# New step lists and PSUM rooms for a gated linear attention and its maxout layer

## Chip, core and metric

The kernel runs on one core of a Trainium2 chip. The metric is the device time of one launch in microseconds (us). "The median" is that of the runs shown.

## What is computed

Four batches, eight heads, 768 positions, head dimension 48. The attention is a recurrence with a complex gate for each position and channel; its output, turned into 3072 rows of 384, goes through three matrices of 384 x 768, an elementwise maximum and a matrix of 768 x 384. The inputs are float32, the four matrices float64.

```python
mag = np.sqrt(a_re * a_re + a_im * a_im)
scale = np.minimum(mag, 0.999) / (mag + 1e-06)
a_re_n, a_im_n = (a_re * scale, a_im * scale)
for t in range(S):
    ar, ai = (a_re_n[:, :, t, :, None], a_im_n[:, :, t, :, None])
    new_re = ar * S_re - ai * S_im
    new_im = ar * S_im + ai * S_re
    kv = np.einsum('bhd,bhe->bhde', k[:, :, t], v[:, :, t])
    S_re, S_im = (new_re + kv, new_im)
    y[:, :, t] = np.einsum('bhd,bhde->bhe', q[:, :, t], S_re)
...
h = np.maximum(np.maximum(x @ w1, x @ w2), x @ w3)
return (h @ w_out).astype(np.float32)
```

## The kernel before, in words

The recurrence is computed in chunks. A chunk x is 128 positions of one batch with all eight heads; two chunks, called x and y in the step names, form a pair, and there are twelve pairs, 0 to 11. A pair goes through the gates, the scores, the state and the output of the attention, then through the maxout layer and the output matrix. Several pairs are in work at the same time.

All work is cut into steps, and the order of the steps is one list, SCHEDULE, written out by hand or by a planner ahead of time. A word such as `tpqx:5` is a step's name and its pair. The loop `program` calls `run` on each word; each engine gets its instructions in the order of the list, held by manual dependencies (class Bound), so an engine never overtakes itself. The engines still wait for one another's results.

The steps that matter here:

- L.. are loads issued by SyncE (Lr and Li the gate's parts, Lk, Lq, Lv; WL the weights). W with a, b, c, e, g turns float64 weights into float32: a on ScalarE, b, c, e on VectorE, g an accumulating transfer of GpSimd.
- sqr, sqi, add, lnL, expe, expw, lne, relu, Lnop, abs, pw, addw, lnw, expL, mulai, mulw, stt, xor, half, atan and turn make the gate's logarithm and angle on ScalarE and VectorE. Lnop and addw are either accumulating transfers of GpSimd or additions on VectorE. Activations of two table sets alternate, and each change of the set is a table load on ScalarE.
- cs, sums and F are TensorE's running sums of angles and logarithms. t, nf, af, sa and sb turn the angles into sines; En, Ek, Eq and f0 to f3 are exponentials out of PSUM on ScalarE.
- mk, mq, uk, uq and kEn scale k and q on VectorE; tpk and tpq are TensorE's transposes, 16 matmuls each; Kc and Qc copy them out of PSUM. Q1, Q2, QB, KB and QG are further factors on VectorE.
- A and B are score matmuls; g0 to g3 (VectorE) and b0, b1 (ScalarE) put the scores under a mask. dk is the state's matmuls, h0 to h3 add it up. y is the output in PSUM, the steps xx and xy copy it to the tile xhx.
- For pair 0 the maxout layer runs plainly (U01x and so on, O). From pair 1, U01, U11, U02 and U12 are nine matmul blocks each (width 256), and u01 to u12 take the maximum on VectorE, with the first as a relu on either engine. The output matrix uses seven products (Strassen) P1 to P7: S1 to S4 are sums on VectorE, Px and Py a remaining block, and r1, r6, r75, r57, ox and oy collect the products into the tile ot. Dx and Dy store it.

TensorE works with five shapes of its array, here called tiles: 128x128 for up, op, pw, wt and wm; 128x64 for cs; 128x32 for A, B and y; 64x128 for tp; 64x64 for F, sums and dk. In the profile's names "up" are the U steps, "op" the products P and O.

PSUM is used as four rooms of two banks. Each step of TensorE takes the next room from the string SLOTS (digits 0, 2, 4, 6); it waits until what stood there has been read. The set OTHER names the steps made by the other engine of ScalarE and VectorE than usual.

Of the kernel before, what the change touches and what calls it, by code (L numbers as in the profile page):

```python
# [26 lines left out]
turn1:0 nfx:0 Wc9:0 afx:0 Wa10:0 T2:0 sqr:1 sqi:1 sax:0 sbx:0 t2:0 Wc10:0 We9:0 add:1 ukx:0 WL11:0 Lvx:0 uqx:0 We10:0
csy:0 tpkx:0 tpqx:0 lnL:1 ty:0 Kcx:0 Eqy:0 expw:1 kEnx:0 xor:1 nfy:0 Lky:0 Liy:2 Lix:2 WL1:0 WL2:0 Lrx:2 WL4:0 Lvy:0
Lry:2 dkx:0 Fy:0 Wb11:0 relu:1 Qcx:0 expe:1 QBx:0 Q2x:0 mqy:0 abs:1 Wa11:0 Wc11:0 Wb1:0 half:1 lne:1 f2y:0 Eny:0 f1y:0
Eky:0 f3y:0 h1x:0 f0y:0 pw:1 Wa1:0 lnw:1 expL:1 We11:0 Wb2:0 Q1x:0 h2x:0 Wc1:0 h3x:0 QGx:0 Wa2:0 afy:0 say:0 mulai:1  # L30
We1:0 CL:0 Wb4:0 Wc2:0 mulw:1 We2:0 M0:0 M1:0 Zg:0 Lnop:1 Cdx:0 Wg1:0 Cdy:0 Wa4:0 sby:0 sqr:2 sqi:2 sumsx:1 Ax:0 M2:0
Wg2:0 stt:1 Wc4:0 mky:0 atan:1 uqy:0 Ekx:1 Eqx:1 Enx:1 We4:0 add:2 lnL:2 expe:2 relu:2 g0x:0 g1x:0 uky:0 KBx:0 g2x:0
g3x:0 turn:1 m1:0 Bx:0 b0x:0 tpqy:0 tpky:0 m0:0 b1x:0 Kcy:0 WL5:0 Lkx:1 csx:1 csy:1 tx:1 yx:0 xor:2 Qcy:0 Wb5:0 nfx:1
Q2y:0 Q1y:0 ty:1 expw:2 afx:1 Wa5:0 xx:0 abs:2 Ay:0 sax:1 QBy:0 Wc5:0 KBy:0 We5:0 addw:2 kEny:0 nfy:1 g0y:0 g1y:0 g2y:0
g3y:0 Wg4:0 Z4:0 Wg5:0 half:2 Cdx:1 Z3:0 WL7:0 WL8:0 Lqx:1 Lqy:1 Lky:1 U11x:0 sumsy:1 dky:0 By:0 lnw:2 Wb7:0 QGy:0
u11x:0 expL:2 mulai:2 mulw:2 Eny:1 Eky:1 Eqy:1 b0y:0 Wa7:0 h1y:0 b1y:0 afy:1 U02x:0 U01x:0 yy:0 u01x:0 xy:0 sbx:1 say:1
sby:1 h2y:0 Wc7:0 Cdy:1 Z2:0 Lvx:1 h3y:0 stt:2 U12x:0 Liy:3 atan:2 lne:2 We7:0 u12x:0 mkx:1 mqx:1 u02x:0 ukx:1 turn:2
mky:1 uqx:1 Wb8:0 U01y:0 U02y:0 U11y:0 u11y:0 u01y:0 U12y:0 Wa8:0 u02y:0 u12y:0 uky:1 csx:2 tx:2 nfx:2 tpkx:1 tpqx:1
tpky:1 Lnop:2 Wc8:0 We8:0 Wg7:0 Kcx:1 Kcy:1 Qcx:1 U21y:0 Fx:1 sumsx:2 Fy:1 Lix:4 f3x:1 f1x:1 f2x:1 f0x:1 f3y:1 f1y:1
f2y:1 f0y:1 u21y:0 csy:2 kEnx:1 Q1x:1 Wg8:0 ty:2 Eqx:2 Ekx:2 U21x:0 u21x:0 Enx:2 mqy:1 uqy:1 Q2x:1 nfy:2 U22y:0 dkx:1  # L40
tpqy:1 Qcy:1 afy:2 say:2 h0x:1 h1x:1 QBx:1 Ax:1 g0x:1 u22y:0 KBx:1 g1x:1 Lqx:2 Lky:2 Lvy:1 Lkx:2 Lix:3 h0y:1 mqx:2 h2x:1
Q2y:1 h3x:1 Q1y:1 g2x:1 g3x:1 sbx:2 sqi:3 sby:2 afx:2 Oy:0 Fx:2 oy:0 sax:2 Bx:1 b1x:1 b0x:1 Ay:1 QGx:1 yx:1 Lvx:2 Lrx:3
Lry:3 Lqy:2 U22x:0 kEny:1 QBy:1 g0y:1 g1y:1 g2y:1 KBy:1 g3y:1 f2x:2 f3x:2 xx:1 sqr:3 sumsy:2 Eqy:2 f0x:2 f1x:2 add:3
u22x:0 dky:1 By:1 Ox:0 J3:0 mkx:2 h1y:1 b1y:1 Eny:2 Eky:2 lnL:3 expe:3 b0y:1 relu:3 h2y:1 ukx:2 mky:2 uqx:2 xor:3 uky:2
QGy:1 expw:3 ox:0 abs:3 tpkx:2 tpqx:2 kEnx:2 h3y:1 yy:1 Kcx:2 Qcx:2 xy:1 dkx:2 Fy:2 addw:3 mqy:2 Q2x:2 half:3 QBx:2
f1y:2 f0y:2 f3y:2 lne:3 lnw:3 expL:3 f2y:2 uqy:2 h0x:2 KBx:2 Q1x:2 U11:1 u11:1 mulw:3 h1x:2 J1:0 Lnop:3 tpky:2 tpqy:2
kEny:2 Ax:2 Kcy:2 Qcy:2 Lrx:4 Lry:4 Lvx:3 Liy:4 Dx:0 Lvy:2 U01:1 Q1y:2 g0x:2 g1x:2 g2x:2 Q2y:2 g3x:2 mulai:3 h2x:2 h3x:2
Cdy:2 Cdx:2 sumsy:3 Bx:2 u01:1 Ay:2 Fx:3 KBy:2 g0y:2 g1y:2 h0y:2 b0x:2 b1x:2 Eny:3 g2y:2 stt:3 Eqy:3 sqr:4 atan:3 g3y:2
U02:1 U12:1 QGx:2 QBy:2 J2:0 turn:3 sqi:4 f1x:3 f0x:3 f2x:3 f3x:3 add:4 yx:2 u12:1 u02:1 csx:3 csy:3 lnL:4 xx:2 tx:3
xor:4 S1:1 nfx:3 dky:2 sumsx:3 ty:3 nfy:3 h1y:2 Eky:3 expe:4 Enx:3 Eqx:3 expw:4 S2:1 QGy:2 h2y:2 h3y:2 relu:4 afx:3 S3:1  # L50
By:2 Ekx:3 P5:1 P6:1 P1:1 P7:1 sax:3 sbx:3 Lqy:3 Lqx:3 abs:4 mqx:3 afy:3 b0y:2 b1y:2 say:3 r1:1 sby:3 addw:4 lne:4 Lix:5
Dy:0 Lry:5 Lkx:3 Lvx:4 Px:1 P2:1 S4:1 mkx:3 P3:1 Py:1 J4:0 yy:2 xy:2 r6:1 r75:1 uqx:3 ukx:3 Lky:3 mqy:3 uqy:3 r57:1
mky:3 tpkx:3 tpqy:3 tpqx:3 Lrx:5 Lvy:3 Liy:5 h0x:3 Kcx:3 kEnx:3 P4:1 Qcy:3 lnw:4 Qcx:3 uky:3 dkx:3 Fy:3 U11:2 f1y:3
expL:4 f0y:3 Lnop:4 oy:1 Q2x:3 half:4 mulai:4 mulw:4 f3y:3 f2y:3 h1x:3 QBx:3 Q1x:3 ox:1 stt:4 h0y:3 sqi:5 h2x:3 Q1y:3
Cdx:3 Cdy:3 h3x:3 Dy:1 Dx:1 atan:4 sqr:5 add:5 lnL:5 turn:4 Lix:6 Lqy:4 Lry:6 Lrx:6 Lky:4 Lqx:4 U01:2 u01:2 u11:2 U02:2
tpky:3 Kcy:3 csy:4 expe:5 ty:4 relu:5 xor:5 u02:2 S3:2 QGx:3 csx:4 tx:4 expw:5 abs:5 Ax:3 nfy:4 nfx:4 KBx:3 kEny:3 g0x:3
g1x:3 afx:4 U12:2 u12:2 g2x:3 g3x:3 S1:2 Fx:4 f2x:4 f3x:4 f1x:4 f0x:4 sumsy:4 Eny:4 Eqy:4 Eky:4 Lkx:4 dky:3 Lvy:4 Liy:6
sumsx:4 Bx:3 Ekx:4 Eqx:4 S2:2 Q2y:3 mqy:4 h1y:3 addw:5 sby:4 sbx:4 sax:4 b1x:3 b0x:3 h0x:4 h2y:3 KBy:3 h3y:3 mky:4 QBy:3
mkx:4 ukx:4 P7:2 P6:2 P5:2 P1:2 yx:3 Ay:3 xx:3 lnw:5 lne:5 expL:5 r1:2 Enx:4 Px:2 Py:2 P4:2 QGy:3 S4:2 r6:2 g0y:3 g1y:3
g2y:3 g3y:3 afy:4 mulw:5 r75:2 half:5 P2:2 By:3 P3:2 b1y:3 b0y:3 yy:3 say:4 xy:3 r57:2 mqx:4 uqx:4 ox:2 mulai:5 tpqx:4  # L60
tpkx:4 oy:2 kEnx:4 Fy:4 uky:4 Lnop:5 Kcx:4 uqy:4 sumsx:5 U11:3 KBx:4 Lqx:5 Cdx:4 f2y:4 stt:5 f3y:4 Ekx:5 f0y:4 Lkx:5
Dy:2 Dx:2 Qcx:4 Enx:5 Q1x:4 Cdy:4 u11:3 Eqx:5 QBx:4 mkx:5 QGx:4 U01:3 atan:5 Q2x:4 u01:3 f1y:4 h0y:4 U02:3 u02:3 sqr:6
dkx:4 h1x:4 sqi:6 h2x:4 h3x:4 Fx:5 f0x:5 f3x:5 add:6 f1x:5 f2x:5 Ax:4 g0x:4 Lqy:5 g1x:4 Bx:4 lnL:6 expe:6 g2x:4 g3x:4
U12:3 lne:6 b1x:4 tpky:4 turn:5 mqx:5 b0x:4 tpqy:4 Qcy:4 u12:3 kEny:4 S1:3 csy:5 ty:5 csx:5 Kcy:4 dky:4 nfy:5 S3:3
sumsy:5 h1y:4 h2y:4 tx:5 nfx:5 h3y:4 afy:5 yx:4 Eky:5 Eny:5 Eqy:5 afx:5 Q2y:4 Q1y:4 sbx:5 P5:3 P1:3 P7:3 Lky:5 sax:5
Ay:4 xx:4 KBy:4 ukx:5 uqx:5 Lrx:7 tpqx:5 S2:3 expw:6 relu:6 QBy:4 Lnop:6 mky:5 tpkx:5 S4:3 Kcx:5 g0y:4 Qcx:5 P6:3 Px:3
Py:3 r1:3 By:4 P2:3 P4:3 say:5 sby:5 QGy:4 g1y:4 abs:6 g2y:4 g3y:4 b1y:4 b0y:4 KBx:5 mqy:5 r6:3 r75:3 r57:3 kEnx:5 oy:3
Q1x:5 uky:5 xor:6 Lry:7 sqr:7 Fy:5 f2y:5 sumsx:6 uqy:5 f3y:5 yy:4 P3:3 ox:3 f0y:5 Lkx:6 xy:4 QGx:5 addw:6 U11:4 Liy:7
Dx:3 QBx:5 Ekx:6 mkx:6 Enx:6 Lvx:5 f1y:5 lnw:6 Lqx:6 h0y:5 u11:4 Q2x:5 expL:6 mulai:6 mulw:6 U01:4 u01:4 tpky:5 h0x:5
Eqx:6 Kcy:5 tpqy:5 stt:6 Ax:5 Lix:7 atan:6 g0x:5 Qcy:5 g1x:5 g2x:5 Bx:5 kEny:5 g3x:5 b0x:5 Q2y:5 U02:4 sqi:7 b1x:5 add:7  # L70
lnL:7 relu:7 expe:7 u02:4 U12:4 Fx:6 f2x:6 S3:4 f3x:6 half:6 turn:6 f0x:6 u12:4 Lvy:5 dky:5 h1y:5 Q1y:5 f1x:6 sumsy:6
dkx:5 Eny:6 csy:6 csx:6 h1x:5 mqx:6 S1:4 Dy:3 ty:6 nfy:6 S2:4 Eqy:6 Lqy:6 mqy:6 Eky:6 P1:4 KBy:5 tx:6 nfx:6 afx:6 lne:7
expw:7 afy:6 P7:4 abs:7 Lky:6 Ay:5 QBy:5 g0y:5 g1y:5 g2y:5 yx:5 g3y:5 addw:7 sbx:6 sax:6 ukx:6 uqx:6 By:5 say:6 P5:4
xx:5 P6:4 r1:4 r6:4 lnw:7 xor:7 S4:4 half:7 Px:4 P2:4 b0y:5 Py:4 r75:4 P4:4 r57:4 P3:4 expL:7 mulw:7 QGy:5 oy:4 tpqx:6
tpkx:6 b1y:5 Lnop:7 mky:6 Qcx:6 Q1x:6 ox:4 Liy:8 kEnx:6 yy:5 sumsx:7 xy:5 Cdx:6 Enx:7 Fy:6 f2y:6 f0y:6 f3y:6 mulai:7
f1y:6 Eqx:7 QBx:6 QGx:6 Q2x:6 stt:7 Lqx:7 Ekx:7 Lix:8 U01:5 sqi:8 Lry:8 Cdy:6 Kcx:6 Lrx:8 Lvx:6 dkx:6 h1x:6 sby:6 mqx:7
# [966 lines left out]
```

## Time and profile before

| | |
|---|---|
| median of three runs | 557.37 us (556.8 to 559.04) |
| span of the profiled execution, first to last instruction | 553.2 us |
| median less that span | 4.2 us |
| TensorE busy | 523.6 us |
| VectorE busy | 482.1 us |
| ScalarE busy | 368.2 us |
| mean granted clock of TensorE | 0.992 |
| table loads of ScalarE | 49, 62.9 us in all |

The profile shows one execution. Its own time is known by the span, to which the time of launch and end is to be added. A row of a timeline has start, length, engine, line, operation, out<-in, shapes and a count; in square brackets stands the idle time ahead of it and what ended that. Almost every row carries line 201, that of the helper which records the instructions, so rows are told apart by their tiles. A matmul in float32 leaves two records. The rows of matmuls overlap, so distances are taken from start to start.

### The profile page before, as it was taken

Reading aid. Unit: us, or ns where it says so; the run is one execution under the profiler, and the core shown is the slowest. Engines: PE = TensorE matmul, PEld = TensorE weight load, DVE = VectorE, ACT = ScalarE, POOL = GpSimd, SP = SyncE. Lnnn points to the kernel's source line nnn. Section 1 sums busy time; section 2 is a strip of 40 time slices with the busy share of each in tenths; the row PEclk is TensorE's granted clock in tenths of the full one; section 3 lists DMA queues with packets and bytes.
Section 4 is the critical chain, followed back from the end, with each engine's and each line's share of the span. In section 5 each row is a group of like instructions: output and inputs, shape, how many; then the busy total and the mean of one; then the engine's idle time right before and its main releaser. Section 6 shows DMA issues by size and latency. Waiting matters only on the chain.

```text
span 553.2 us, 22687 instructions
## 1 busy us (share of the span) xinstructions
PE 523.6 (95%) x10086; PEld 448.1 (81%) x10086; DVE 482.1 (87%) x752; ACT 368.2 (67%) x653; POOL 70.8 (13%) x113
## 2 busy tenths in 40 slices
...
GB/s 203 295 246 176 174 131 79 50 128 63 109 38 124 67 68 51 61 44 88 72 121 58 35 85 108 101 91 54 62 125 20 32 105 72 2 31 2 31 1 28
...
## 3 DMA queue, kind: packets, MB, share of 16 engines
...
q14 instruction: 18, 0.15, 0.1%
...
## 4 chain that ended last, share of the span: by engine, by line
PE 84%; DVE 7%; ACT 4%; SPq 2%; issue 1%; DMA 1%; DVEq 0%; ACTq 0%
PE up L201 33%; PE op L201 24%; PE y L201 7%; PE A L201 5%; PE tp L201 4%; PE dk L201 3%; PE sums L201 2%; PE cs L201 2%; DVE w L201 2%; SPq L201 2%; PE F L201 2%; PE B L201 1%; DMA wo<-in_moe_w_dram 1%; DVE atm L201 1%; ACT f L201 1%
## 5 line engine op out<-in xcount | busy, mean ns | idle before, releaser
L201 PE MATMUL up<-xhx,w 128*128 128x256 f32 x792 | 177.0, 382 | 0.1
L201 PEld LDWEIGHTS up<-xhx,w 128*128 128x128 f32 x792 | 148.6, 190 | 21.5 <-PE B L201 0.3
L201 ACT ACT_TABLE_LOAD x49 | 62.9, 1283 | 1.6 <-PEq L1027 0.8
L201 ACT COPY atm<-B 32x128 f32<-32x128 f32 x96 | 24.6, 256 | 37.8 <-DVE atm L201 19.7
L201 PE MATMUL op<-wo,xhx 128*128 128x192 f32 (+1 forms) x220 | 48.4, 363 | 0.0
L201 DVE TENSOR_TENSOR Q<-Q,f 112x1024 f32<-112x1024 f32 (+1 forms) x48 | 45.4, 952 | 1.7 <-ACT Q L201 1.2
L201 POOL DMA_DIRECT2D ar<-nf x40 | 34.6, 1305 | 60.3 <-DVE ar L201 48.9
L201 ACT ACTIVATE f<-F 48x232 f32<-48x232 f32 x96 | 34.5, 359 | 10.1 <-PE F L201 6.1
L201 PEld LDWEIGHTS op<-wo,xhx 128*128 128x128 f32 x220 | 36.5, 190 | 4.6 <-issue 0.6
L201 PE MATMUL y<-atm,vb 128*32 128x64 f32 x1152 | 39.0, 221 | 0.2 <-ACT K L201 0.2
L201 PE MATMUL y<-QG,g 112*32 112x64 f32 x1408 | 38.0, 219 | 0.2 <-issue 0.2
L201 PEld LDWEIGHTS y<-atm,vb 128*32 128x32 f32 x1152 | 32.4, 109 | 5.3 <-issue 2.9
L201 PEld LDWEIGHTS y<-QG,g 112*32 112x32 f32 x1408 | 34.8, 109 | 0.3 <-issue 0.3
L201 DVE TENSOR_TENSOR ot<-ot,op 128x384 f32<-128x384 f32 (+1 forms) x56 | 25.6, 464 | 10.7 <-PE op L201 6.4
L201 PE MATMUL op<-wo,strassen 128*128 128x192 f32 x176 | 33.0, 331 | 0.0
L201 POOL DMA_DIRECT2D Ln<-e x9 | 8.3, 923 | 192.2 <-ACT e L201 53.8
L201 PE MATMUL A<-Q,K 112*32 112x80 f32 x1536 | 31.6, 234 | 1.4 <-DVE Q L201 1.4
L201 DVE COPY_PREDICATED atm<-masko,A 128x256 f32<-128x256 uint8 x72 | 31.2, 435 | 1.7
L201 PE MATMUL op<-w,strassen 128*128 128x192 f32 x176 | 32.2, 329 | 0.0
L201 PEld LDWEIGHTS A<-Q,K 112*32 112x32 f32 x1536 | 27.3, 110 | 4.2 <-issue 3.1
L201 PEld LDWEIGHTS op<-wo,strassen 128*128 128x128 f32 x176 | 28.8, 190 | 0.8
L201 ACT COPY Q<-tp 112x1024 f32<-112x1024 f32 x22 | 22.3, 1014 | 10.7 <-PE tp L201 10.5
...
## 6 DMA issues: line engine op xcount, KB each, us to landing
...
Ln<-e POOLq DMA_DIRECT2D x9, 384.0 KB, 4.1
w<-L POOLq DMA_DIRECT2D x7, 384.0 KB, 4.4
```

Of the source, the lines that this page charges most:

```text
L201: ins = f(*a, **kw)
```

## The change

The list SCHEDULE keeps its 1,880 words and has them in another order. SLOTS keeps its 304 digits, in another order. In the new order TensorE changes its tile 163 times instead of 190. OTHER loses 27 names and gets 36. Three places in the code give the list more freedom: t may be made by VectorE (five times it is), r1 may be made by VectorE (six times), and P2 and P3, which add into one part of PSUM, may come in either order, with the last of them closing the sum.

The first and the last line of each list, and the code:

```diff
 SCHEDULE = """
-Lrx:0 sqr0:0 Lix:0 sqi0:0 add0:0 lnL0:0 expe0:0 expw0:0 lne0:0 relu0:0 WL0:0 Wb0:0 Liy:0 Wa0:0 sqi1:0 Zf:0 Lry:0 sqr1:0
...
-r6:10 b0y:11 Px:10 P2:10 Py:10 P4:10 QGy:11 b1y:11 r75:10 r57:10 oy:10 yy:11 xy:11 P3:10 ox:10 Dx:10 U12:11 U01:11
-u01:11 U11:11 U02:11 u11:11 u12:11 P1:11 S3:11 Dy:10 u02:11 S1:11 S2:11 Px:11 P2:11 P5:11 S4:11 P6:11 r1:11 r6:11 Py:11
-P3:11 P7:11 r75:11 ox:11 P4:11 Dx:11 r57:11 oy:11 Dy:11
+Lrx:0 sqr0:0 Lix:0 Zf:0 sqi0:0 add0:0 xor0:0 lnL0:0 expe0:0 Lry:0 expw0:0 lne0:0 relu0:0 Lnop0:0 Liy:0 sqi1:0 sqr1:0
...
+U12:11 u11:11 u12:11 P6:10 r1:10 r6:10 r75:10 r57:10 S3:11 U01:11 u01:11 P3:10 U02:11 u02:11 P7:11 ox:10 P1:11 S1:11
+P5:11 Px:11 Dx:10 r1:11 oy:10 Py:11 P4:11 S2:11 P6:11 P2:11 S4:11 Dy:10 r6:11 r75:11 r57:11 P3:11 ox:11 Dx:11 oy:11
+Dy:11
 """
...
 OTHER = set("""
-Zf:0 Zg:0 afx:0 relu:1 Qcy:0 addw:2 Lnop:2 Wg8:0 u21y:0 addw:3 relu:4 afx:3 abs:4 Lnop:4 u01:2 xx:3 afy:4 afx:5 addw:6
...
-Kcx:10 Qcy:10 Kcy:11 Kcx:11 xy:11 u01:11 u11:11
+Zf:0 afx:0 relu:1 Zg:0 u21y:0 Wg8:0 relu:3 abs:3 ty:3 afy:3 xy:2 tx:4 ty:4 u01:2 Qcy:3 relu:5 afy:4 Lnop:5 u11:3 u01:4
...
+afx:10 xy:9 Kcy:10 Lnop:11 u01:9 afx:11 afy:11 Qcy:11 Qcx:11 xy:11 u11:11 r1:10 u01:11 r1:11
 """.split())
...
         elif name == "t":
             T["t", x] = turned["t"][c]
-            activation(out=T["t", x], in_=T["cs", x], func=AF.Copy, scale=-1.0, bias=MAGIC)
+            if other():
+                dve.tensor_scalar(out=T["t", x], in0=T["cs", x], scalar1=-1.0, scalar2=MAGIC, op0=OP.mult, op1=OP.add)
+            else:
+                activation(out=T["t", x], in_=T["cs", x], func=AF.Copy, scale=-1.0, bias=MAGIC)
...
             left = {1: a11, 2: a12, 3: s1, 4: a22, 5: s1, 6: s2, 7: s3}[i]
+            last = i not in (2, 3) or ("half", g) in T
+            if i in (2, 3):
+                T["half", g] = i
             for n in range(4):
                 mm(out=r[i], lhsT=left[:, n], rhs=factor(i)[:, (n + 2 * (g % 2)) % 4],
-                   start=i in (1, 5, 6, 7) and n == 0, stop=i != 2 and n == 3)
+                   start=i in (1, 5, 6, 7) and n == 0, stop=last and n == 3)
...
             if name == "r1":
-                act.copy(out=xl, in_=r[1])
+                copy(out=xl, in_=r[1])
```

More of the change, by code (lines that the diff above doesn't have):

```diff
@@ L27 @@
[L27 to L76, printed above, removed]
@@ L87 @@
-dky:7 S1:6 h1y:7 h2y:7 csx:8 csy:8 tx:8 ty:8 nfy:8 h3y:7 afy:8 yx:7 xx:7 P7:6 relu:9 expw:9 KBy:7 say:8 sby:8 Lqy:8 P1:6
-S2:6 P6:6 nfx:8 Q1y:7 QBy:7 Lky:8 mky:8 By:7 afx:8 uky:8 sbx:8 Ay:7 abs:9 Lnop:9 tpky:8 Lrx:10 QGy:7 g0y:7 g1y:7 g2y:7
-sax:8 Kcy:8 P5:6 S4:6 g3y:7 ukx:8 r1:6 uqx:8 mqy:8 r6:6 h0x:8 b0y:7 r75:6 r57:6 b1y:7 Px:6 P2:6 P3:6 Py:6 P4:6 kEny:8
-tpkx:8 ox:6 oy:6 addw:9 lnw:9 tpqx:8 yy:7 Qcx:8 sumsx:9 Kcx:8 kEnx:8 xy:7 Fy:8 Q1x:8 sumsy:9 Enx:9 xor:9 f1y:8 f0y:8
-expL:9 half:9 mulai:9 Cdy:8 f2y:8 f3y:8 Eny:9 Liy:10 mulw:9 QGx:8 stt:9 U11:7 KBx:8 Eky:9 uqy:8 Lry:10 sqr:10 Lqx:9
@@ new lines @@
+sumsx:1 dkx:0 h1x:0 KBy:0 QGx:0 yx:0 Q2y:0 Enx:1 afx:1 Q1y:0 Eqx:1 Wa5:0 Ekx:1 xx:0 afy:1 h2x:0 Lix:3 Lqy:1 Lkx:1
+Lvy:0 WL7:0 Wb7:0 Ay:0 addw:2 QBy:0 half:2 Cdy:1 Wa7:0 lnw:2 lne:2 g0y:0 Wc5:0 g1y:0 h3x:0 g2y:0 dky:0 h1y:0 By:0
+U01x:0 expL:2 We5:0 Wg5:0 Cdx:1 g3y:0 b0y:0 b1y:0 Wc7:0 QGy:0 u01x:0 sby:1 U11x:0 yy:0 xy:0 h2y:0 mulw:2 sumsy:1 Lvx:1
+mulai:2 sbx:1 u11x:0 say:1 h3y:0 WL8:0 Lqx:1 stt:2 sax:1 We7:0 mqx:1 atan:2 turn:2 U01y:0 mkx:1 Eqy:1 uqx:1 Wb8:0
+U11y:0 u11y:0 U12y:0 u12y:0 u01y:0 Fx:1 U02y:0 Eny:1 Eky:1 csx:2 csy:2 f3x:1 f0x:1 f1x:1 mky:1 f2x:1 Wa8:0 ukx:1 uky:1
@@ new lines @@
+expw:4 ty:3 U02:1 nfx:3 expe:4 afx:3 nfy:3 Q1y:2 relu:4 abs:4 lne:4 S3:1 u02:1 Ax:2 g0x:2 Ay:2 Bx:2 g1x:2 Lqy:3 g2x:2
+g3x:2 b1x:2 b0x:2 h0x:2 KBy:2 Lnop:4 S1:1 dkx:2 h1x:2 h2x:2 P7:1 P1:1 QBy:2 P5:1 g0y:2 g1y:2 g2y:2 g3y:2 addw:4 lnw:4
+Dy:0 Lix:5 Lvy:2 Lkx:3 yx:2 xx:2 By:2 r1:1 b1y:2 h3x:2 QGy:2 J4:0 S2:1 b0y:2 sqr:5 Liy:5 dky:2 sumsx:3 h1y:2 expL:4
+mulw:4 half:4 Cdy:3 mulai:4 Px:1 P2:1 P6:1 r6:1 Ekx:3 Enx:3 Py:1 P4:1 sqi:5 Eqx:3 h2y:2 stt:4 atan:4 yy:2 sax:3 afy:3
+mqx:3 S4:1 P3:1 sby:3 say:3 xy:2 U11:2 h3y:2 mkx:3 add:5 r75:1 ox:1 r57:1 Cdx:3 turn:4 csx:4 Dx:1 sbx:3 uqx:3 oy:1
@@ new lines @@
+g0y:3 g1y:3 g2y:3 Lkx:4 mkx:4 mqx:4 kEny:3 yx:3 g3y:3 Dy:1 r6:2 QGy:3 h0y:3 xx:3 Cdx:4 Px:2 Py:2 P4:2 P2:2 By:3 Liy:6
+r75:2 dky:3 h1y:3 sbx:4 sax:4 b1y:3 r57:2 P3:2 uqx:4 Lqx:5 mulw:5 oy:2 ox:2 h2y:3 h3y:3 mulai:5 stt:5 b0y:3 yy:3 sby:4
+xy:3 tpqx:4 Qcx:4 Fx:4 f1x:4 afy:4 sumsy:4 Eqy:4 Fy:4 f0y:4 f0x:4 f3y:4 Dy:2 f2x:4 f3x:4 Eky:4 f2y:4 f1y:4 Lnop:5 Dx:2
+Lky:4 Lry:6 Lvy:5 Eny:4 atan:5 sqr:6 U11:3 u11:3 say:4 ukx:4 Q2x:4 QBx:4 QGx:4 sqi:6 turn:5 add:6 lnL:6 mky:4 mqy:4
+U12:3 U01:3 u12:3 uky:4 Lky:5 U02:3 u01:3 tpky:4 expe:6 lne:6 uqy:4 tpqy:4 tpkx:4 h0x:4 Q1x:4 Kcy:4 u02:3 S1:3 kEnx:4
```

130 lines of the change are left out of this document (86 added, 44 removed).

## The prediction

> **What bounds the kernel now.** I read the page first, for shares. The chain that ended last lies 84% on TensorE, which is busy for 95% of the span.
>
> ```profile
> PE 523.6 (95%) x10086; PEld 448.1 (81%) x10086; DVE 482.1 (87%) x752; ACT 368.2 (67%) x653; POOL 70.8 (13%) x113
> ...
> PE 84%; DVE 7%; ACT 4%; SPq 2%; issue 1%; DMA 1%; DVEq 0%; ACTq 0%
> ```
>
> A share over the whole span hides stages, so next came the busy time by stretches (columns: PE, PEld, DVE, ACT, POOL, then clock and DMA).
>
> ```profile
> 0.00:70.00 70.00, 45.98 (x718) 31.31 (x719) 61.45 (x104) 64.05 (x111) 26.70 (x62) 0.95 0.90 218
> 70.00:105.00 35.00, 34.62 (x784) 29.51 (x786) 34.41 (x57) 28.02 (x54) 4.86 (x6) 1.00 0.56 98
> 105.00:500.00 395.00, 394.67 (x7957) 344.15 (x7950) 362.13 (x553) 273.06 (x479) 39.28 (x47) 1.00 0.37 71
> 500.00:553.20 53.20, 48.34 (x659) 43.18 (x650) 24.06 (x41) 3.06 (x11) 0.00 (x0) 0.99 0.05 16
> ```
>
> There are three stages. Until 70 us VectorE and ScalarE are nearly full and TensorE loses 24 us. From 105 to 500 us TensorE is without a gap. At the end TensorE loses some 5 us. The waits of TensorE, first from 100 to 549 us, then until 105 us (its two longest), say the same:
>
> ```profile
> PE op L201 <- DVE ot L201: 1.2, 1, 1.2
> PE y L201 <- issue: 0.2, 1, 0.2
> ...
> PE F L201 <- DVE Ln L201: 9.8, 1, 9.8
> PE tp L201 <- DVE uk L201: 3.4, 1, 3.4
> ```
>
> From 105 us on only TensorE's own stream can be shortened, apart from one wait at the end. A busy TensorE is not one that streams: what lies between two groups of matmuls counts as busy too, and there the change acts.
>
> **The change part by part: fewer changes of tile.** In TensorE's order I counted neighbouring groups with another tile (128x128: up, op, pw, wt, wm; 128x64: cs; 128x32: A, B, y; 64x128: tp; 64x64: F, sums, dk): 189 before and 162 after, with the same 5,436 matmuls; the first group makes it the named 190 and 163. Those that leave 128x128 fall from 60 to 53, those that leave a smaller tile from 129 to 109. The price is the start of the next group after equal groups, once without a change of tile and once with one. In the timeline of TensorE (start, length):
>
> ```profile
> 98.52 0.46 PE L201 MATMUL B<-QB,KB 112*32 112x32 f32 x32
> 98.80 0.33 PE L201 MATMUL A<-Q,K 112*32 112x80 f32 x6
> ...
> 236.74 0.56 PE L201 MATMUL F<-cuts,Ln 64*48 64x29 f32 x32
> 237.12 0.37 PE L201 MATMUL sums<-Ln,mid 64*64 64x192 f32 x4
> ...
> 280.35 0.52 PE L201 MATMUL F<-cuts,Ln 64*48 64x29 f32 x32
> 280.80 0.48 PE L201 MATMUL up<-xhx,w 128*128 128x256 f32 x1
> ...
> 506.95 0.46 PE L201 MATMUL B<-QB,KB 112*32 112x32 f32 x32
> 507.34 1.57 PE L201 MATMUL op<-wo,xhx 128*128 128x192 f32 x8
> 508.74 1.46 PE L201 MATMUL op<-w,strassen 128*128 128x192 f32 x8
> 510.04 1.46 PE L201 MATMUL op<-wo,strassen 128*128 128x192 f32 x8
> 511.43 0.26 PE L201 MATMUL y<-atm,vb 128*32 128x64 f32 x4
> ```
>
> Eight op matmuls take 1.30 us to the next op (508.74 to 510.04) and 1.39 us to y: 0.09 us for leaving 128x128. B takes 0.28 us to A and 0.39 us to op: 0.11 us. F takes 0.38 us to sums and 0.45 us to up: 0.07 us. The dearest is dk:
>
> ```profile
> 211.21 1.08 PE L201 MATMUL dk<-vb,uk 64*64 64x48 f32 x62
> 212.08 0.23 PE L201 MATMUL F<-cuts,Ln 64*48 64x29 f32 x2
> ...
> 404.57 1.11 PE L201 MATMUL dk<-vb,uk 64*64 64x48 f32 x64
> 405.62 0.48 PE L201 MATMUL up<-xhx,w 128*128 128x256 f32 x1
> ```
>
> It takes 0.87 us to F and 1.05 us to up: 0.18 us. For the packed tiles I take the mean of the three, 0.12 us less a little because dk is rare (11 of the 109 changes that remain): 7 x 0.09 + 20 x 0.115 = 2.9 us; the ends are 27 x 0.07 = 1.9 us and 27 x 0.18 = 4.9 us.
>
> The Trainium skill bears on this twice. "TensorEngine Tiling (Array Packing)", Key Properties, states that another tiling mode, not merely another tile, drains TensorE; the rows above agree. "TensorE: Matmul & The Clock Gate", Single matmul latency, gives a lone matmul a fixed part of about 166 ns, where a stream overlaps it; if each change cost all of that, the estimate would be 27 x 0.166 = 4.5 us instead of 2.9 us. The op rows show little more than half of it.
>
> **The end.** Before, P4 of the last pair stands behind ox in the list and writes the two-bank tile that ox reads (the row of VectorE at 546.81 holds r75, ox and r57).
>
> ```profile
> 546.81 1.41 DVE L201 TENSOR_TENSOR ot<-ot,op 128x384 f32<-128x384 f32 x3 [2.50 <-PE op L201]
> 548.01 1.57 PE L201 MATMUL op<-w,xhx 128*128 128x192 f32 x8 [1.23 <-DVE ot L201]
> 549.61 0.62 DVE L201 TENSOR_TENSOR ot<-ot,op 128x192 f32<-128x192 f32 x2 [1.40 <-PE op L201]
> ```
>
> After, P4 comes early, all products stand ahead of ox, and P3 is last. The 1.23 us of idling goes. P3 needs S4, which needs S2 and the end of P5; between P5 and P3 stand Px, Py, P4, P6 and P2, so this is covered. What is late next is ox, now behind the last matmul as a third add there: 1.41 / 3 = 0.47 us. So 1.23 - 0.47 = 0.76 us are gained, and I take 0.7 us, since ox's store is now issued just ahead of the last ones. The ends are 0 (the third add and its store cost all of it) and 1.2 us.
>
> **The start.** Here VectorE and ScalarE set the pace, so I compared which steps stand ahead of yy of pair 0 (TensorE's second y, at 71.44 us) in the two lists. Ahead before but no longer: for TensorE one sums and U02x; for VectorE mulai and mulw of pair 2; for ScalarE four activations of 384 elements, a small relu and two table loads (seven up to the copies b1y, now five). Newly ahead: Wc7 on VectorE; lne of pair 2 (768 elements), one activation of 384 and a small relu on ScalarE. The durations:
>
> ```profile
> 61.75 0.56 DVE L201 TENSOR_SCALAR xhx<-xhx 128x768 int32<-128x768 int32 x1
> 63.69 0.95 DVE L201 TENSOR_TENSOR w<-w,L 128x768 f32<-128x768 f32 x1
> ...
> 62.62 1.60 PE L201 MATMUL up<-ot,w 128*128 128x128 f32 x12
> 64.15 0.56 PE L201 MATMUL sums<-Ln,mid 64*64 64x192 f32 x8
> 64.53 0.51 PE L201 MATMUL sums<-Ln,rest 64*64 64x192 f32 x8
> ...
> 71.44 0.43 PE L201 MATMUL y<-atm,vb 128*32 128x64 f32 x16
> ...
> 64.12 1.28 ACT L201 ACT_TABLE_LOAD   x1
> 65.42 0.84 ACT L201 ACTIVATE L<-w 128x768 f32<-128x768 f32 x1
> ```
>
> VectorE has 2 x 0.95 - 0.56 = 1.3 us less ahead of that y. ScalarE's activations come out about even, and it has 2 x 1.28 = 2.6 us less in table loads. TensorE has 1.53 + 0.7 = 2.2 us less done by then (from start to start, the two overlapping rows of sums together). If VectorE sets the pace, y comes 1.3 us earlier and leaves 2.2 us more: 0.9 us lost. If ScalarE does, 0.4 us are gained; if neither saving counts, 2.2 us are lost. I take 0.4 us lost, between the two engines and nearer to VectorE, which ended both waits of TensorE shown above; the ends are 0.4 us gained and 2.2 us lost.
>
> **Moved sides and queues.** Counted by kind, VectorE makes 761 instructions instead of 752: fewer copies of K and adds of w, more copies of r1, xhx and t. At the 0.95 us of a full row above, nine more are at most 8.6 us. ScalarE loses table loads (49 to 43) and copies. I cost both at nothing: from 105 us TensorE's 394.67 us stand against VectorE's 362.13 us, so 32 us cover the 8.6 us, which would be lost without them. GpSimd issues two more accumulating transfers:
>
> ```profile
> w<-L POOLq DMA_DIRECT2D x7, 384.0 KB, 4.4
> ```
>
> In the list they stand further ahead of their readers than before; without that distance each would cost its landing, 4.4 us. SyncE's loads also stand earlier; a load whose buffer is still read holds up the stores queued behind it, but the next pair's r1, which waits for those, comes a whole pair later.
>
> **Sum.** 2.9 + 0.7 - 0.4 = 3.2 us of a span of 553.2 us. What lies around the span is the same for both, 4.2 us against the median of 557.37 us. That gives 554.2 us.
>
> **The rivals.**
>
> *VectorE's pace eats part of it.* Up to 105 us VectorE is busy for 34.41 of 35 us, and 11 of the 27 changes that go lie in TensorE's work from its 50th to its 100th us (25 before, 14 after), a good part of which is done in that stretch. If VectorE sets the time there, only 16 x 0.107 = 1.7 us remain: 1.7 + 0.7 - 0.4 = 2.0 us, so 555.4 us. For it: that busy share. Against it: TensorE shows hardly any wait from 70 us on.
>
> *Each change costs what dk shows.* 4.9 + 0.7 - 0.4 = 5.2 us: 552.2 us. For it: the dk rows, and 20 of the 27 leave packed tiles. Against it: B, F and op. By the Trainium skill's 166 ns the same sum would give 552.6 us.
>
> *PSUM's four rooms run full: slower.* The new list has seven runs of four transpose steps (64 matmuls) where the old has one (pair 11). Such a run takes all four rooms, so the next step waits for a copy out of the first. The old one, with its copies on ScalarE:
>
> ```profile
> 485.71 0.48 ACT L201 COPY xhx<-y 128x384 f32<-128x384 f32 x1 [2.75 <-PE y L201]
> 486.28 1.02 ACT L201 COPY Q<-tp 112x1024 f32<-112x1024 f32 x1
> ...
> 487.51 0.48 PE L201 MATMUL up<-xhx,w 128*128 128x256 f32 x1
> ```
>
> The copy ends at 487.30, up starts at 487.51: a cover of 0.2 us. One table load and one activation ahead of the copy (1.28 and 0.84 us, the rows above) take 2.1 us, thus 1.9 us of stall a run; six new runs make 11.4 us, and 554.2 + 11.4 = 565.6 us. It decides from 3.2 / 6 = 0.53 us a run, when a copy is 0.7 us late. For it: the thin cover. Against it: ScalarE is busy for 273 of 395 us and in that row had idled 2.75 us; in the list the first copy stands right behind its transposes. The Trainium skill's "TensorEngine Tiling (Array Packing)", PSUM Bottleneck, warns that tiling speeds up TensorE and not the emptying of PSUM, which would be this case.
>
> **How the numbers follow.** About 0.5%, 2.8 us, is what a measurement of this kernel can tell from no change; my forecast lies just beyond it. Forecast 0.55 (0.42 beyond the bound, 0.13 within, since the ends reach across it: its own range goes from 2.9 + 1.2 + 0.4 = 4.5 us gained, 552.9 us, to 2.9 + 0.7 - 2.2 = 1.4 us, 556.0 us), VectorE's pace 0.20 (within), dear changes 0.10 (faster), full rooms 0.15 (0.14 slower, 0.01 within). So faster 0.52, same 0.34, slower 0.14. The range runs from 551.8 us, just below the dear changes, to 558.0 us, where full rooms cost 0.6 us a run and have eaten all the gain.
>
> **What would show it.** Right: from 105 us to the last stretch TensorE has no waits over 0.3 us; op to y still 1.39 us; TensorE's last wait on ot gone, and three adds behind the last matmul; the second y of pair 0 near 70 us. Wrong: waits of TensorE on K or Q behind runs of 64 transposes, more than 0.5 us each; gaps ended by VectorE between 70 and 150 us; y of pair 0 beyond 72 us.

## The result and the profile after

The changed kernel is slower: 578.88 us median of four runs (576.51 to 582.66) against 557.09 us for the kernel before on the same chip, a ratio of 1.0385 with a 95% interval of 1.0335 to 1.0434. The profiled execution has a span of 574.8 us; its own time was 576.51 us. The forecast of 554.2 us went the wrong way, and the time lies far outside its range.

The page of the changed kernel, busy times and the chain that ended last:

```profile
PE 527.6 (92%) x10086; PEld 451.9 (79%) x10086; DVE 482.5 (84%) x761; ACT 356.4 (62%) x636; POOL 71.3 (12%) x115
...
q8 instruction: 79, 1.29, 0.9%
...
PE 77%; DVE 7%; DMA 7%; issue 5%; ACT 2%; SPq 1%; POOL 0%; DVEq 0%; ACTq 0%
```

TensorE makes the same 10,086 records of matmuls in about the same busy time (527.6 us against 523.6), in a span that is 21.6 us longer. In the chain DMA has grown from 1% to 7%, and "issue", the profile's name for time in which an engine waited for nothing that it shows, from 1% to 5%. By stretches (columns as before):

```profile
0.00:70.00 70.00, 44.42 (x678) 28.14 (x678) 56.13 (x97) 59.76 (x106) 26.33 (x63) 0.85 0.91 218
70.00:105.00 35.00, 30.64 (x543) 25.83 (x543) 29.05 (x46) 25.55 (x49) 5.63 (x6) 0.95 0.49 92
105.00:500.00 395.00, 383.50 (x7846) 336.38 (x7848) 354.59 (x554) 259.49 (x455) 39.37 (x47) 1.00 0.38 72
500.00:574.80 74.80, 69.05 (x1030) 61.55 (x1020) 42.72 (x67) 11.58 (x28) 0.00 (x0) 1.00 0.05 18
```

Two stages lost. By 105 us TensorE had started 1,221 records of matmuls (678 + 543), where before it had started 1,502; its 1,503rd starts 10.5 us later (115.49 us against 105.02 in the two traces). And the long middle stretch, which had no gap, now has 11.5 us in which TensorE is idle. In the start VectorE waits for loads (waits of VectorE up to 115 us: total, times, longest):

```profile
DVE xhx L203 <- DMA strassen<-in_moe_w_dram: 6.7, 1, 6.7
DVE q L203 <- DMA q<-in_q_dram: 5.9, 1, 5.9
```

In the middle TensorE waits for nothing that is named (waits of TensorE from 105 us on, the seven longest sums):

```profile
PE A L203 <- issue: 2.4, 3, 1.6
PE y L203 <- issue: 2.3, 3, 1.5
PE op L203 <- issue: 1.9, 2, 1.1
PE F L203 <- issue: 1.8, 2, 1.5
PE dk L203 <- issue: 1.2, 2, 1.0
PE B L203 <- issue: 1.1, 1, 1.1
PE sums L203 <- issue: 0.7, 1, 0.7
```

These are 11.4 us in all. Before, the same view has none; the one row of the kind in the prediction, 0.2 us, stands ahead of 105 us, at 100.67 us. None of the rows names ACT K or ACT Q, the copies out of PSUM that I had feared, and the wait on ot is gone.

Such a gap can lie in the middle of a group, where no step waits for another. Timeline of TensorE:

```profile
483.57 0.46 PE L203 MATMUL B<-QB,KB 112*32 112x32 f32 x32
483.85 1.34 PE L203 MATMUL A<-Q,K 112*32 112x80 f32 x64
485.11 1.02 PE L203 MATMUL dk<-vb,uk 64*64 64x48 f32 x55
487.10 0.33 PE L203 MATMUL dk<-vb,uk 64*48 64x48 f32 x9 [0.96 <-issue]
```

Operands and room of dk were there: 55 of its matmuls had run. Three packed groups (many small matmuls on parts of the array) stand side by side, 151 records of matmuls start within 2.6 us, and then TensorE stands still. What these places have in common shows when instructions are counted from the end of one gap to the end of the next (stretches; the first two counts are matmuls and weight loads):

```profile
111.50:119.90 8.40, 7.31 (x255) 5.98 (x254) 5.53 (x11) 3.74 (x10) 0.89 (x1) 1.00 0.64 112
119.90:156.13 36.23, 35.40 (x635) 29.70 (x636) 32.48 (x49) 22.23 (x35) 5.94 (x7) 1.00 0.55 106
156.13:193.65 37.52, 35.16 (x635) 30.35 (x634) 31.64 (x47) 22.70 (x40) 3.34 (x4) 1.00 0.31 56
193.65:242.33 48.68, 48.31 (x1016) 43.57 (x1017) 45.07 (x72) 32.04 (x59) 5.91 (x7) 1.00 0.42 82
```

The sums are 509, 1271, 1269 and 2033. With the semaphore instructions of TensorE's own queue, which these counts leave out, they are 512, 1280, 1280 and 2048: 2, 5, 5 and 8 times 256. Counted from the first instruction, 16 of the 17 gaps over 0.3 us end at number 193 to 200 of a block of 256; this place is called a boundary here. (The sums of gaps from here on, 16.6 us for after, are taken from the start of one matmul to the next, less the usual step of its group; how that step is taken moves them by up to about a tenth.) And 79 packets on queue q8 carry 1.29 MB, 16 KB each. The trace holds 20,330 instructions of TensorE (2 x 10,086 and 158 of its queue), and from number 194 on, every 256, they cross 79 boundaries: one packet for each. So q8 brings TensorE's program, 256 instructions a packet. For three gaps, the times of the packets in the trace against the boundaries (us):

```
boundary crossed   next packet starts, ends   next boundary reached   from packet's end   gap there
     106.47             109.21  110.26              111.58                  1.32             1.7
     189.85             191.28  192.17              193.74                  1.57             1.8
     483.76             484.57  485.88              487.09                  1.22             1.2
```

A packet starts 1.1 us (median) after TensorE crosses a boundary, takes about 1 us, and over the whole trace no boundary is crossed sooner than 1.2 us after its packet ended. By these three a block that TensorE could run in less than some 3.3 us (an estimate) ends in a gap. It is no sharp bound: 14 of the 79 packets start ahead of their crossing, by up to 4.5 us, and four blocks of after run in 2.3 to 2.4 us without a gap, each with a packet that starts at its crossing or ahead of it. Why some start early the trace doesn't show. This theory of the instruction supply is what the experiments had to test; the rivals were a wait of another kind that belongs to these places of the order, and transfers that crowd out the packets.

### The profile page after: what moved, and what is told of

Read it like the earlier page. It is cut to its first block, busy times and chain, and to the rows that moved or that the text cites. A ratio compares the mean times of both kernels' runs of the same rounds, so it can differ in the third digit from the quotient of the medians.

```text
span 574.8 us, 22659 instructions
## 1 busy us (share of the span) xinstructions
PE 527.6 (92%) x10086; PEld 451.9 (79%) x10086; DVE 482.5 (84%) x761; ACT 356.4 (62%) x636; POOL 71.3 (12%) x115
## 3 DMA queue, kind: packets, MB, share of 16 engines
q8 instruction: 79, 1.29, 0.9%
## 4 chain that ended last, share of the span: by engine, by line
PE 77%; DVE 7%; DMA 7%; issue 5%; ACT 2%; SPq 1%; POOL 0%; DVEq 0%; ACTq 0%
PE up L203 29%; PE op L203 22%; PE y L203 6%; PE A L203 4%; PE tp L203 4%; PE dk L203 3%; PE sums L203 3%; PE cs L203 2%; DMA q<-in_q_dram 2%; PE F L203 2%; SPq L203 1%; DMA strassen<-in_moe_w_dram 1%; DMA xhx<-in_moe_w_dram 1%; DMA Ln<-e 1%; DVE xhx L203 1%
## 5 line engine op out<-in xcount | busy, mean ns | idle before, releaser
L203 POOL DMA_DIRECT2D ar<-nf x40 | 36.5, 1294 | 150.5 <-DVE ar L203 140.1
L203 DVE TENSOR_TENSOR Q<-Q,f 112x512 f32<-112x512 f32 (+1 forms) x48 | 44.9, 952 | 2.2 <-ACT f L203 1.3
L203 POOL DMA_DIRECT2D w<-L x10 | 10.8, 1084 | 185.5 <-ACT L L203 117.1
L203 DVE TENSOR_TENSOR QG<-Q,f 112x1024 f32<-112x1024 f32 (+1 forms) x24 | 27.1, 1130 | 5.1 <-PE y L203 3.9
L203 ACT ACTIVATE xhx<-up 128x768 f32<-128x768 f32 x14 | 11.2, 810 | 31.6 <-PE up L203 31.6
```

Source lines behind the costliest of these rows:

```text
L203: ins = f(*a, **kw)
```

## The experiments

**1 and 2: moving the boundaries of the kernel before.** Both add small matmuls ahead of the first transposes, in an idle stretch, and nothing else.

```diff
             ps = banks("tp")
+            for e in range(0 if "extra" in T else EXTRA):
+                o = e % 4 * 32
+                mm(out=ps[o:o + 32, 0, 0:1], lhsT=ident[0:DD, o:o + 32], rhs=ident[0:DD, 0:1], start=True, stop=True)
+            T["extra"] = True
```

> The kernel before with 22 small matmuls (32x1) ahead of the first transposes of pair 0, where TensorE idled 3.5 us at 30.4 us; their results are overwritten. 22 matmuls of two passes are 88 instructions. Theory 'instruction supply': in the trace of after every stall that the profile calls issue stands at instruction 193 to 200 of a block of 256 of TensorE's own stream, and each block comes with one 16 KB packet. 88 instructions more move all later block boundaries to other places of the same order, so that stalls of 0.3 to 1.8 us appear inside packed groups of a kernel that has only two now: 10 to 28 us slower. Rival 'the stalls belong to the places in after's order' (a semaphore, a transfer, a group that follows another): 22 small matmuls cost at most 1 us, and no issue stall appears.

> The same with 64 small matmuls, 256 instructions, one whole block. Instruction supply: the boundaries fall on the same places as before, one block later, so the time is that of before within 2 us, though three times as much was added as with 22. Rival: three times the cost of 22, whatever that is.

Measured: with 22 the ratio to before is 1.0481 [1.0436, 1.0526], 583.45 us, 26.5 us more. With 64 it is 1.0033 [1.0002, 1.0065], 559.15 us, 2.2 us more; the 64 outlast the idle stretch, and the first transposes start 1.9 us later than before (32.35 against 30.43 us). The waits of TensorE from 105 us on, the four largest sums with 22:

```profile
PE B L202 <- issue: 4.9, 4, 1.6
PE F L202 <- issue: 3.7, 3, 1.9
PE y L202 <- issue: 3.6, 3, 2.1
PE A L202 <- issue: 2.7, 2, 1.6
```

and with 64:

```profile
PE op L202 <- DVE ot L202: 1.2, 1, 1.2
PE y L202 <- issue: 1.1, 2, 0.7
```

All gaps over 0.3 us of this kind sum to 24.7 us with 22 small matmuls, and 20 of the 21 end at numbers 193 to 201 of 256. The 22 themselves took 0.8 us. Loads, stores and the order of all steps are those of before, so neither the transfers nor the places of after's order make the gaps: the block boundaries do. It also shows what before's time rests on: its boundaries fall on good places. Of its last 71 full blocks, 3 run in under 3 us; of all stretches of 256 instructions from 70 us on, wherever they begin, 19% do, which would be 13 or 14 of 71. Whether before's order was fitted to that or came to it by luck, no run shows.

**3, 4 and 6: the beginning of one list, the rest of the other.** After 444 of the 1,880 words (about 105 us) the lists differ by six words each, so one list's beginning was joined to the other's rest. Digits of SLOTS and names of OTHER were set anew to go with it.

```diff
 SCHEDULE = """
-(after's list)
+(444 words of before's list, then what is left, in after's order)
```

> The first 444 words of before's list (to about 105 us, where the two lists differ by 6 words each), then the remaining words in after's order. Theory 'two separate losses': the start's loss of some 9 us is gone and the issue stalls after 105 us, some 13 us, stay: 569 us (566 to 573). Rival 'the late start makes the rest': near 557 us. Rival 'all of it is the order after the start': 577 or more.

> The first 444 words of after's list, then the remaining words in before's order. Two separate losses: 566 us (563 to 569), with late loads up to 110 us and next to no issue stalls from 115 us on. Rival 'the late start makes the rest': near 579 us. Rival 'the delay of the start is caught up': near 557 us.

Measured: before's start with after's rest 580.34 us (1.0422 [1.0388, 1.0455]), after's start with before's rest 570.96 us (1.0237 [1.0185, 1.0288]). The first lies where the last rival had put it (577 us or more), but not for that rival's reason: the seam made a wait that neither kernel has. ScalarE in the timeline of that run:

```profile
120.55 0.84 ACT L203 ACTIVATE L<-w 128x768 f32<-128x768 f32 x1 [5.94 <-DMA w<-L]
```

A transfer (addw of pair 3) that stands 16 words ahead of the cut in after's list came behind the cut here and was late, and TensorE lost 11.3 us at the seam; beyond it 13 us of issue gaps remain, most of them at the places of after's. The second run is 2 us beyond its forecast of 563 to 569 us: around its seam, from 114 to 133 us, three boundary gaps (4.4 us) and a wait on VectorE (1.3 us) stand. From 137 us on its only wait of TensorE is that on ot (1.2 us). So from there before's order has no such gaps behind after's start either, and the late start is not caught up.

The seam was to be mended by issuing that transfer earlier. In this run it adds L to w of pair 3 before the magnitudes of pair 3 are written to L, so that pair's gates come out of other numbers; the steps are the same.

```diff
-... expw:3 ox:0 abs:3 tpkx:2 tpqx:2 kEnx:2 Fy:2 addw:3 lnw:3 h3y:1 mqy:2 uqy:2 half:3 ...
+... expw:3 addw:3 ox:0 abs:3 tpkx:2 tpqx:2 kEnx:2 Fy:2 h3y:1 mqy:2 uqy:2 lnw:3 half:3 ...
```

> As the run with the start of before, but with the transfer addw of pair 3 right behind expw of pair 3 and its logarithm six words later: in that run VectorE and ScalarE waited 6 us on it at 115 to 124 us, a wait that neither kernel has and that came from the seam of the two lists. Theory 'start and block boundaries are two losses': 570 us (567 to 573), with some 13 us of issue stalls left. Rival: 577 or more, if after's steady order loses time in another way than at block boundaries.

Measured: 575.74 us (1.0325 [1.0278, 1.0371]), between the two numbers. TensorE still lost 8 us at the seam, and some 11 us in issue gaps behind it. Neither hybrid with before's start isolates the start; the next run does.

**5: after with early loads.** Only seven words of loads move within SyncE's queue.

```diff
-We4:0 ... Lix:3 Lqy:1 Lkx:1 Lvy:0 WL7:0 Wb7:0 ... We5:0 ... Lvx:1 ... WL8:0 Lqx:1 stt:2
+We4:0 WL7:0 Lvy:0 Lkx:1 Lqx:1 Lqy:1 ... Wb7:0 ... We5:0 WL8:0 ... Lvx:1 Lix:3 ... stt:2
```

> After, with seven loads at other places of SyncE's queue and nothing else moved: block 7 of the weights (strassen) right behind the step that frees its room, then v of pair 0's second half, k, q and q of pair 1, block 8 right behind its room's last step, and the a_im load of pair 3 behind them. Theory 'late loads make the start's loss': the waits of 6.7 us on strassen and 5.9 us on q on VectorE, and 1.6 us of TensorE on vb, go; 5 to 10 us faster than after (569 to 574 us). Rival 'the order of TensorE's groups and of VectorE's steps makes it': within 2 us of after (577 to 581).

Measured: 568.59 us (1.0209 [1.015, 1.0268] to before), 10.3 us below after. What had happened shows in SyncE's queue of after (timeline: start and length of the issue):

```profile
59.40 1.24 SPq L203 DMA_DIRECT2D strassen<-in_moe_w_dram  x1
...
71.52 0.38 SPq L203 DMA_DIRECT2D xhx<-in_moe_w_dram  x1
71.94 3.70 SPq L203 DMA_DIRECT2D q<-in_q_dram  x4
```

and in VectorE's timeline of the same kernel:

```profile
66.79 0.56 DVE L203 TENSOR_SCALAR xhx<-strassen 128x768 f32<-128x768 f32 x1 [6.67 <-DMA strassen<-in_moe_w_dram]
83.19 0.56 DVE L203 TENSOR_TENSOR q<-Eq,q 128x384 f32<-128x384 f32 x1 [5.88 <-DMA q<-in_q_dram]
```

Weight block 7 (strassen) stood in the queue behind a_im of pair 3 and q, k and v, 13 issues most of which were needed later, and went out at 59.40 us. Block 8 (xhx) waits for its room; q of pair 1 stood behind it and went out at 71.94 us. Before issues them at 51.89 and 64.22 us:

```profile
51.89 0.95 SPq L201 DMA_DIRECT2D strassen<-in_moe_w_dram  x1
...
64.22 7.00 SPq L201 DMA_DIRECT2D q<-in_q_dram  x8
```

With the early loads they leave at 50.71 and, from 57.57 us on, ahead of block 8 (SyncE's timeline of that run):

```profile
50.71 0.37 SPq L203 DMA_DIRECT2D strassen<-in_moe_w_dram  x1
...
57.57 7.21 SPq L203 DMA_DIRECT2D q<-in_q_dram  x8
```

and TensorE's timelines have pair 0's second y, of that run and then of after:

```profile
70.07 0.43 PE L203 MATMUL y<-atm,vb 128*32 128x64 f32 x16
...
74.71 0.43 PE L203 MATMUL y<-atm,vb 128*32 128x64 f32 x16
```

It begins at 70.07 us; in after it began at 74.71. TensorE's lower granted clock in the start of after (0.85 up to 70 us, against 0.95 before) is not what delays it: run 5 has the same 0.85. TensorE's 1,503rd record comes at 106.61 us instead of 115.49. The gaps over 0.3 us that are not "issue" fall from 21.6 to 10.7 us; those of "issue" stay (16.6 and 17.2 us). So these are two separate losses.

**7: moving the boundaries of after.** The edit of the first run, with 24 small matmuls, in after.

> After with 24 small matmuls (96 instructions) ahead of its first transposes. Instruction supply: the 17 issue stalls leave their places and others come, at places 96 instructions earlier in the order modulo 256; worked out from the times between its instructions, with 3.5 us as the least time from one block boundary to the next, the stalls sum to some 30 us in place of 17: 589 us (583 to 595). Rival 'after's stalls belong to its places': the same 17 stalls, 579 to 581 us.

Measured: 593.62 us (1.0642 [1.059, 1.0694]), within the forecast. The issue gaps sum to 29.3 us, and 19 of the 23 end at numbers 193 to 201 of 256, at other steps than in after. The forecast from the boundaries was 30 us. From 105 us on, the three largest waits of TensorE:

```profile
PE B L204 <- issue: 8.3, 5, 2.2
PE y L204 <- issue: 5.0, 4, 1.5
PE dk L204 <- issue: 4.5, 4, 2.0
```

**8 and 9: before with its last 23 words in the order of after's end.**

```diff
-... P1:11 S3:11 Dy:10 u02:11 S1:11 S2:11 Px:11 P2:11 P5:11 S4:11 P6:11 r1:11 r6:11 Py:11 P3:11 P7:11 r75:11 ox:11 P4:11 Dx:11 r57:11 oy:11 Dy:11
+... P1:11 S3:11 Dy:10 u02:11 S1:11 Px:11 P7:11 P5:11 r1:11 Py:11 P4:11 S2:11 P6:11 P2:11 S4:11 r6:11 r75:11 r57:11 P3:11 ox:11 Dx:11 oy:11 Dy:11
```

> Before with only its last 23 words in another order: P7, P5 and P4 of the last pair earlier, P3 and the add ox behind the combinations, as in after. The wait of TensorE of 1.2 to 1.4 us on VectorE's ot goes and one more add of 0.47 us follows the last matmul: 0.5 to 0.9 us faster than before, if no block boundary is moved into a bad place (the number of instructions ahead is the same). Rival: the order of P1 to P7 makes a new wait on S1 to S4, and it is 0 to 1 us slower.

> Before with the last 23 words as in the run of the tail, and 5 small matmuls (20 instructions) ahead of the first transposes. Instruction supply, worked out from the times between the instructions with about 3.6 us as the least time from one boundary to the next: a shift of 16 to 24 instructions is the best of the 64 possible ones for this order, and takes the issue stalls that are left (1.9 us in the run of the tail) to under 0.5 us; five matmuls cost 0.1 to 0.2 us. So 0.3 to 1.5 us faster than the run of the tail, 554 to 556 us, though it makes more instructions. Rival: more work is more time, 0.1 to 0.5 us slower than the run of the tail.

Measured: the end alone gives 555.85 us (0.9979 [0.9953, 1.0004]), 1.3 us below before's 557.12; the interval just reaches 1. The wait on ot is gone; the only row of the waits from 105 us on is

```profile
PE y L203 <- issue: 1.2, 2, 0.8
```

With five small matmuls on top it is 558.87 us (1.0042 [1.002, 1.0064]), 3 us more: the forecast missed, and so did the rival's 0.1 to 0.5 us. The issue gaps did not go, they summed to 2.7 us in place of 2.0, one of them (1.0 us) in a group of up; what makes the rest of the 3 us stays open. Worked out with one least time for all blocks, the rule gave the 30 us of run 7 well, but not the last one or two microseconds.

**10: spreading after's packed groups.** From the times between TensorE's instructions in run 5, 115 of its steps were moved by up to 8 places so that the blocks take longer, with the other engines' orders kept.

```diff
 SCHEDULE = """
-(the list of run 5, TensorE with 162 changes of tile between its groups)
+(115 of TensorE's steps moved by at most 8 places, 183 changes of tile)
```

> The kernel with the seven early loads, with 115 of TensorE's steps moved by at most 8 places so that 256 instructions take longer than the least time at each boundary; the other engines' orders are kept, PSUM's rooms handed out anew. The number of changes of tile goes from 162 back to 183. Instruction supply: issue stalls fall from 17 us to some 6 us, 21 changes of 0.11 us cost 2.3 us, and a few us of moved steps are late for their readers: 3 to 8 us faster than the run with the early loads (560 to 565 us). Rival 'fewer changes of tile is the gain, and stalls come from elsewhere': 2 us slower or more, 571 us and up.

Measured: 578.73 us (1.0384 [1.0348, 1.042]), 10 us slower than run 5 and where the rival had put it. The issue gaps fell only from 17.2 to 14.5 us, and gaps of other kinds rose from 10.7 to 20 us. Some of them, from 105 us on:

```profile
PE tp L202 <- DVE uq L202: 2.6, 1, 2.6
...
PE up L202 <- ACT En L202: 1.6, 1, 1.6
...
PE up L202 <- DVE xhx L202: 0.8, 1, 0.8
```

As soon as one step comes at another time, the times at which later blocks run change as well, and steps moved on one engine alone are late for the others. So it neither bears out the rival nor settles what after would take without its gaps. That fewer changes of tile go with quick blocks it does show: to lengthen the quick blocks on paper took 21 of the 27 changes back.

**11: the sides alone.** Before's list with after's set OTHER.

```diff
 OTHER = set("""
-(before's 45 names)
+(after's 54 names)
```

> Before's list and rooms with after's choice of sides (27 names out, 36 in: copies, magnitudes, adds and the like between ScalarE, VectorE and GpSimd's accumulating transfers). Theory 'moved sides cost nothing': within 1.5 us of before, no new wait of TensorE over 0.5 us after 105 us. Rival 'the moved sides are part of the loss': VectorE's nine more instructions, up to 8.6 us, and copies that come late: 560 to 566 us.

Measured: 613.05 us (1.1018 [1.0983, 1.1053]). TensorE waits for GpSimd's accumulating transfers, issued too late in before's order, and for VectorE (waits over the whole run):

```profile
PE up L203 <- DMA w<-w: 14.9, 2, 10.4
PE F L203 <- DVE Ln L203: 9.1, 1, 9.1
```

Neither theory fits. Sides and order belong together; the price of the sides within after's own order cannot be had by this exchange and stays open. In after's own trace no wait of TensorE on another engine or on a transfer is over 0.6 us from 105 us on.

**12: the price of a change of tile.**

```diff
                 b = ALONG[g % 2][3 * f + j]
+                if g == NG - 1:
+                    n = 32 if j % 2 == i % 2 else P
+                    mm(out=ps[0:n, j, 0:1], lhsT=ident[:, 0:n], rhs=ident[:, 0:1], start=True, stop=True)
```

> Before with twelve small matmuls in the last four groups of up, one ahead of each run of three 128x256 matmuls: six on a tile of 128x32 (two changes of tile each) and six on 128x128 (none). Their results are overwritten. It measures the price of a change by itself: the time from the last matmul of one run to the first of the next, small tile less large tile, is two changes. Theory 'a change costs 0.09 to 0.12 us, whichever tile': 0.18 to 0.24 us. Rival 'dear changes', as dk shows: 0.36 us. Rival 'changes are free in a stream': under 0.05 us. The whole run: 1 to 3 us above before.

Measured: 558.74 us against 555.6, one run of each, so these two times decide nothing. TensorE's timeline:

```profile
523.84 1.54 PE L201 MATMUL up<-xhx,w 128*128 128x256 f32 x6
525.31 0.22 PE L201 MATMUL up<-ident 128*32 128x1 f32 x2
525.47 1.56 PE L201 MATMUL up<-xhx,w 128*128 128x256 f32 x6
526.87 0.28 PE L201 MATMUL up<-ident 128*128 128x1 f32 x2
527.00 1.54 PE L201 MATMUL up<-xhx,w 128*128 128x256 f32 x6
```

From one up to the next it takes 1.63 us (523.84 to 525.47) past a small tile and 1.53 us (525.47 to 527.00) past a large one: two changes cost 0.10 us, less than expected and twice the bound of "free". Nearly all of it is the start of the small tile after 128x128: between the last matmul of up and it lie 0.309 us, against 0.216 us with a large tile.

## Why the prediction was wrong, by its own steps

Two of its steps failed: the sum has no term for TensorE's supply of instructions, and the loads in SyncE's queue stand in it at nothing.

**Fewer changes of tile, 2.9 us gained.** This step holds. From its 1,503rd record to its last, TensorE takes 444.2 us before (105.02 to 549.25) and 454.7 us after (115.49 to 570.19); less the gaps over 0.3 us (2.1 and 14.9 us) that is 442.1 and 439.8 us, and 440.1 us in run 5, which has after's order on TensorE. So the stream is 2.0 to 2.3 us shorter, with 128 changes there in place of 151. In the same stretch, over the usual step of a group, a change that leaves 128x128 takes 0.095 us before and 0.093 after (I had taken 0.09), and one that leaves a smaller tile 0.15 us, where a new group on the same tile takes 0.03: 0.12 us for the change (I had taken 0.115). Run 12 agrees with the first (0.093 us); a lone small matmul, unlike a full group, costs next to nothing to leave.

**The gain was taken as if nothing but operands could stop TensorE.** That is the term that is missing from the sum: 16.6 us of issue gaps, where before has 0.7 us. The prediction showed the row "PE y <- issue: 0.2" and passed over it; it stands at a block boundary of before. Of after's last 71 full blocks, 12 run in under 3 us without their gap, against 3 before. Two things add up there: stretches of 256 instructions that run so fast are more frequent, 25% against 19%, as packed groups stand side by side, and the boundaries avoid them less well. The larger part is the second, as run 1 shows: before's own order loses 24.7 us when its boundaries are moved by 88 instructions.

The Trainium skill, "Runtime: NRT & Kernel Launch", Instruction fetch mechanics, says that instructions come in blocks of 16 KiB, 256 of them, and that crossing into the next one is mostly hidden. The 79 packets of 16 KB agree with the first; the second does not hold for packed groups here, where a crossing cost up to 1.8 us in after and 2.3 us in run 1.

**The start, 0.4 us lost.** This step failed by far: it compared which steps of TensorE, VectorE and ScalarE stand ahead of the second y, and came to 70 us for it. With the loads moved forward it begins at 70.07 us; in after it began at 74.71, beyond the 72 us that were named as a sign of error. The step itself was sound for the engines and left out SyncE.

**Moved sides and queues, at nothing.** Here the reason for the start's loss was costed away. The text looked at a load that holds up stores, a pair later. What stood behind were loads, needed at once: run 5 puts their order at 10.3 us. VectorE, which sets the pace there, waited 6.7 and 5.9 us for them. Accumulating transfers of GpSimd made one wait of TensorE over 1 us in after (1.3 us, at 81 us). The sides by themselves remain open (run 11).

**The end, 0.7 us gained.** Right in its mechanism: TensorE's wait on ot is gone. From the start of the last matmul to the end of the span it now takes 4.6 us (570.19 to 574.8) instead of 3.9 (549.25 to 553.2). Of the 0.7 us more, the third add is 0.46 us, as estimated (three adds take 1.08 us, two took 0.62); the rest comes behind the adds. Against the wait of 1.23 us, some 0.5 us are left. In before's order alone the new end was worth 1.3 us in the medians, with an interval that does not exclude nothing.

**The sum.** Up to the 1,503rd record after is 10.5 us late; run 5, with the early loads, is 1.6 us late. From there to the last, gaps take 12.8 us more (14.9 us against 2.1; 12.9 us of after's are issue gaps) and the stream 2.3 us less, so 10.5 us. Behind the last matmul it is 0.7 us more. Together that is 21.7 us, and the span is 21.6 us longer. The 4.2 us that the prediction put around the span joined a median to the span of one execution; where both stand for one execution of before, they are 2.0 to 2.1 us apart. The forecast, a difference, does not hang on it.

**The rivals.** PSUM's full rooms, the slower one, did not come about: from 105 us on no row of TensorE's waits in after names K or Q. VectorE's pace as worked out did not decide either; VectorE did set the time in the start, but by waiting for loads. Dear changes would need 0.18 us for every change; the stretch above has 0.12 us for leaving a packed group, and run 12 has 0.10 us for two. None of them named a slower case with the right mechanism.

Open are the time that after's order would have without gaps at its boundaries, and what its sides cost. The lowest median found is that of run 8, 555.85 us, with an interval that just reaches before's time.
